# All four experts by pairs of chunks with seven block products, and the conversion steps spread along the experts

## The chip, the cores and the metric

The kernel runs on one core of one Trainium2 chip. The metric is the device time of one execution, in microseconds (us). The engines have the names of the profile: PE (matrix multiplication), PEld (its loading of stationary operands), DVE (vector engine), ACT (activation engine), POOL (GpSimd), and SP, whose queue issues nearly all transfers of this kernel.

## The reference, cut to what matters

```python
def reference(...):
    x = _attn_ref(q, k, v, n_global, n_local)      # banded attention, then [B*S, H*D] = [1536, 512]
    # experts: E = 4, D = 512, F = 1024
    p = domain_probs / (domain_probs.sum(-1, keepdims=True) + 1e-09)
    for e in range(E):
        h = np.maximum(x @ w1[e], 0.0)
        out += p[:, e:e + 1] * (h @ w2[e])
    # gate
    a = out @ w1_; b = out @ w2_
    return ((a * b) @ w3) @ w_out
```

All of it is fp32. The weights of the gate (w_ab, w3t, w_out) come to the kernel as 64-bit words that the kernel itself converts to fp32.

## The kernel before

**Products.** Every fp32 operand is split into a high and a low part (`split`, L48: ACT writes the high part, L50; DVE or POOL subtracts it to get the low one, L51). A product of two operands is three matmuls (`three`, L54: high by high, high by low, low by high, L56 to L58), each with a stationary block of 128x128 and 512 moving columns.

**Stages.** Attention comes first, then the experts, then the product of w3 with w_out, then the gate. The change is in the experts stage and in the conversion that runs beside it.

**The experts.** The 1536 tokens are three chunks c of 512, F is eight blocks f of 128. The loop over `work` (L831 on) takes steps (e, c, f): an up product of 12 matmuls into one of four `z` buffers, relu on ACT (L598) and its low part on DVE (L599), then the down product of the step before the last (`LAG` = 2), 12 matmuls into four `o` buffers that stay open over the eight f. After the eighth f the four `o` buffers are evacuated: DVE multiplies each by the shares of the expert (L804 or L807), and for a later expert POOL adds the result to `acc` (L808). The next group of downs can't start before that. Experts 0 and 1 (`EARLY` = 2) have all three chunks in `work`; experts 2 and 3 have chunk 0 there, 64 steps in all.

**The pairs.** Chunks 1 and 2 of experts 3 and 2, in that order, are done by `Pairs.run` (L705 to L740), one unit for two blocks f and both chunks: eight units n = 0 to 7. The 2x2 block product of a unit is made from seven products P1 to P7 of 6 matmuls each, where eight would be needed directly, from sums of x (made once, L654) and sums of weights (made for each unit, four DVE operations at L700, called the sums below, and their split with the low parts on POOL). The sums of the products are seven DVE adds that read `z` (L707) and one ACT copy (L719). In the program the unit stands as P1, P2, down group D0, P3, P4, D1, P5, D2, P6, D3, P7. The four `z` buffers go round, so a product takes the buffer of the fourth product before it. `prep(0)` after P2 splits the raw weights of the next unit (low parts on POOL), `prep(1)` after P4 makes its sums, `prep(2)` splits the second half of the weights on DVE (not for the first expert of the pairs). `out` writes relu and its low part for four results of the unit. A unit inside an expert has two downs of 12 matmuls (in D0 and D2), so 42 + 24 = 66 matmuls; one that starts another expert (n = 4) has the last two downs of chunk 1 in D0 and the eight of chunk 2 in D1, D2, D3, so 42 + 120 = 162, and evacuates twice.

**The conversion.** Forty pieces of 512 words by 128 partitions. For each: fetch of the raw words (SP), `abs` on ACT (L537), max on POOL (L539, one input), four DVE operations (L545, L548, L551, L553), an add of two inputs on POOL (L554), and the transfer of the result back to device memory. One step of each piece in flight is taken per work step from n = 5 on, with three raw buffers; all of it ends in the work loop.

**Order.** All five engines run in the order in which the program issues (`ORDERED`): an instruction that waits holds up everything behind it on its engine, and an issue of a transfer on SP that waits for its buffer holds up later ones.

## Time and profile before

| | us |
|---|---|
| median of 3 runs (lowest, highest) | 821.35 (821.28, 822.04) |
| the profiled execution | 820.91 |
| its span in the trace | 818.7 |
| PE busy in it | 812.0 (99%) |
| DVE, POOL, ACT busy in it | 507.7 (62%), 318.1 (39%), 283.4 (35%) |
| work loop after attention, 81.5 to 415.9 of the span | 334.4 |
| the eight units of the pairs, 415.9 to 557.3 | 141.4 |

Times of rows are microseconds from the start of the span. A row of the timeline has the start, the duration (from the first to the last of the instructions counted behind the x), the engine, the line, the operation, what it writes and reads, and in brackets how long the engine had been idle before it and what ended that. PE's granted clock is 1.00 in all 40 slices of the span.

### The profile page before, as it was taken

The numbers are of one execution on the slowest core, as the hardware profiler recorded it, in microseconds if no ns is written. First come the engines' busy times: TensorE is split into PE (matmuls) and PEld (weight loads), VectorE is DVE, ScalarE is ACT, GpSimd is POOL, SyncE is SP. The second block draws the span as 40 slices with busy tenths as digits, with TensorE's granted clock in tenths as the row PEclk, the third lists the DMA queues.
The fourth block names the chain that finished last, engine by engine and source line by source line (L and its number), as shares of the span: only waits on it lengthen the run. The fifth ranks groups of instructions, "written<-read, shape, count | busy, mean of one in ns | idle before, by whom it ended". The sixth has DMA issues, their size and how long they took to land.

```text
span 818.7 us, 11030 instructions
## 1 busy us (share of the span) xinstructions
PE 812.0 (99%) x4004; PEld 670.2 (82%) x4005; DVE 507.7 (62%) x945; ACT 283.4 (35%) x591; POOL 318.1 (39%) x320
## 2 busy tenths in 40 slices
PE   9999999999999999999999999999999999999997
PEld 5888888888888888888888888888888888888886
DVE  8996455567655557778648573665543743887850
ACT  7996222124221223333324221332442432333210
POOL 7886034525356464642143351422390003333400
PEclk9999999999999999999999999999999999999999
DMA  9940343558353547643101101121533210201011
GB/s 270 289 124 2 121 143 112 167 161 258 127 162 116 167 151 244 214 139 102 39 26 52 40 26 65 52 65 35 184 103 103 78 52 26 102 27 52 0 46 61
DMA packets 38116, 88.10 MB, mean 108 GB/s; under 512 B 3674, under 2 KB 9866, under 8 KB 38054
## 3 DMA queue, kind: packets, MB, share of 16 engines
q1 hardware_dynamic: 37382, 86.79, 33.4%
q8 instruction: 33, 0.54, 0.3%
q10 hardware_dynamic: 672, 0.54, 0.3%
q14 instruction: 29, 0.24, 0.1%
HBM read 73.66 MB, written 13.66 MB: 107 GB/s over the span
## 4 chain that ended last, share of the span: by engine, by line
PE 97%; DMA 1%; DVE 1%; issue 0%; SPq 0%; ACT 0%; ACTq 0%; DVEq 0%
PE z L56 18%; PE z L58 18%; PE z L57 18%; PE o L57 12%; PE o L58 12%; PE o L56 12%; PE sp L251 2%; PE tp L290 2%; PE op L329 1%; PE op L330 1%; PE tp L177 1%; PE sp L290 1%; DMA wr<-in_w_moe_dram 1%; PE sp L56 0%; PE sp L58 0%; PE sp L57 0%
## 5 line engine op out<-in xcount | busy, mean ns | idle before, releaser
L58 PE MATMUL z<-xh,sl 128*128 128x512 f32 x428 | 166.6, 389 | 0.0
L57 PE MATMUL z<-xl,sh 128*128 128x512 f32 x428 | 166.5, 389 | 0.0
L56 PE MATMUL z<-xh,sh 128*128 128x512 f32 x428 | 166.5, 389 | 0.0
L554 POOL TENSOR_TENSOR cr<-cr,cb 128x512 f32<-128x512 f32 x40 | 51.6, 1290 | 126.6 <-issue 118.8
L58 PEld LDWEIGHTS z<-xh,sl 128*128 128x128 f32 x428 | 80.3, 188 | 17.1 <-DVE sl L51 0.2
L57 PEld LDWEIGHTS z<-xl,sh 128*128 128x128 f32 x428 | 80.3, 188 | 16.7
L56 PEld LDWEIGHTS z<-xh,sh 128*128 128x128 f32 x428 | 80.4, 188 | 16.6
L51 POOL TENSOR_TENSOR sl<-wr,sh 128x512 fp32r<-128x512 f32 (+1 forms) x32 | 32.1, 1024 | 146.5 <-ACT sh L50 146.5
L51 DVE TENSOR_TENSOR sl<-wr,sh 128x1024 fp32r<-128x1024 f32 (+1 forms) x57 | 70.5, 1242 | 23.8 <-ACT sh L50 22.9
L808 POOL TENSOR_TENSOR acc<-acc,t 128x512 f32<-128x512 f32 x36 | 49.2, 1401 | 85.7 <-DVE t L807 85.7
L50 ACT CAST sh<-wr 128x1024 fp32r<-128x1024 f32 (+2 forms) x89 | 70.6, 815 | 22.1 <-PE z L57 10.3
L539 POOL TENSOR_SCALAR ca<-ca 128x512 f32<-128x512 f32 x40 | 61.7, 1543 | 26.8 <-ACT ca L537 26.8
L707 DVE TENSOR_TENSOR t<-t,z 128x512 f32<-128x512 f32 x56 | 37.4, 679 | 32.0 <-PE z L58 27.7
L306 POOL TENSOR_TENSOR pt<-pt,r 128x232 f32<-128x232 f32 (+1 forms) x95 | 48.7, 545 | 8.4 <-DVE r L237 4.4
L56 PE MATMUL z<-sh,sh 128*128 128x512 f32 x120 | 46.7, 389 | 0.0
L57 PE MATMUL z<-sl,sh 128*128 128x512 f32 x120 | 46.7, 389 | 0.0
L58 PE MATMUL z<-sh,sl 128*128 128x512 f32 x120 | 46.7, 389 | 0.0
L277 ACT ACTIVATE pt<-t,negmax 128x232 f32<-128x232 f32 (+1 forms) x96 | 44.8, 473 | 4.5 <-DVE negmax L266 4.4
L51 POOL TENSOR_TENSOR sl<-t,sh 128x256 fp32r<-128x256 f32 (+1 forms) x24 | 23.0, 973 | 31.2 <-ACT sh L50 31.0
L56 PE MATMUL o<-h0h,sh 128*128 128x512 f32 x84 | 32.8, 390 | 0.0
L57 PE MATMUL o<-h0l,sh 128*128 128x512 f32 x84 | 32.7, 389 | 0.0
L58 PE MATMUL o<-h0h,sl 128*128 128x512 f32 x84 | 32.7, 389 | 0.0
(266 smaller groups left out, 1745.4 us busy)
## 6 DMA issues: line engine op xcount, KB each, us to landing
wr<-in_w_moe_dram SPq DMA_DIRECT2D x44, 512.0 KB, 3.4
raw<-in_w3t_dram SPq DMA_DIRECT2D x16, 512.0 KB, 4.0
raw<-in_w_ab_dram SPq DMA_DIRECT2D x16, 512.0 KB, 4.3
wr<-wab_d SPq DMA_DIRECT2D x16, 512.0 KB, 3.3
raw<-in_w_out_dram SPq DMA_DIRECT2D x8, 512.0 KB, 3.4
w3t_d<-cr SPq DMA_DIRECT2D x16, 256.0 KB, 2.5
wab_d<-cr SPq DMA_DIRECT2D x16, 256.0 KB, 2.2
wr<-w3t_d SPq DMA_DIRECT2D x8, 512.0 KB, 3.3
```

The source lines that it names most:

```text
L50: nc.scalar.copy(hi, src)
L51: (lo_engine or nc.vector).tensor_tensor(lo, src, hi.bitcast(F32), op=ALU.subtract)
L56: nc.tensor.matmul(out, wh, xh, start=start, stop=False)
L57: nc.tensor.matmul(out, wh, xl, start=False, stop=False)
L58: nc.tensor.matmul(out, wl, xh, start=False, stop=stop)
L277: nc.scalar.activation(st[u][gr][:, hh, 0:w], t[:, 0:w], AF.Exp, bias=nm, scale=-1.0, accum_out=st[u]["sums"][:, h : h + 1])
L290: nc.tensor.transpose(tp[:, hh, j], pt[:, 2 * half + hh, c], g.ident)
L306: nc.gpsimd.tensor_tensor(pt[:, hh, 0:w], pt[:, hh, 0:w], r[:, hh : hh + 1].to_broadcast([P, w]), op=ALU.mult)
L539: nc.gpsimd.tensor_scalar(a, a, 2.0**-15, None, op0=ALU.max)
L554: nc.gpsimd.tensor_tensor(rest, rest, top.bitcast(F32), op=ALU.add)
L707: add = lambda o, a, b: nc.vector.tensor_tensor(o, a, b, op=ALU.add)
L808: nc.gpsimd.tensor_tensor(acc[c][:, d], acc[c][:, d], t, op=ALU.add)
```

## The change

- `EARLY` is gone: `work` holds chunk 0 of all four experts (32 steps), and the pairs are experts 3, 2, 1, 0, so 16 units n = 0 to 15. Units 4, 8 and 12 start another expert.
- The sums of the weights for the next unit (`prep(1)`) stand before the add of P3 in every unit but 4, 8 and 12 (`early`), where they stay behind the add of P4.
- The conversion is a class, `Convert`, with two raw buffers and operations in place. A step starts a piece (abs, max), sends the result of an earlier one, ends the piece begun before (four DVE operations, POOL add), and fetches the next. The steps stand in a table of places: 12 in the work loop (`CONVERTS`), one inside an `out` of every unit but the last and 4, 8, 12 (`INSIDE`: between relu and its low part), five in each of the units 4, 8, 12 and one more at the end of unit 4 (`BETWEEN`: after a down), and three in the downs after the last unit (`ENDS`).
- Weights of the work steps are fetched up to two slots ahead (`load_more`, `land_until`); in steps 8 to 11 two slots are split per step where one was.
- The sums of x are made in six given work steps (`XSUMS`). For chunks 1 and 2 expert 3 now writes `acc` directly, and expert 0 for chunk 0 as before. A scratch area for transfers is made smaller.

```diff
@@ -35,8 +35,12 @@
 WARM = 10
 FILL = (6, 4)
 W_TILE = 4
-EARLY = 2
 LAG = 2
+XSUMS = (21, 23, 24, 26, 27, 28)
+CONVERTS = (4, 6, 7, 8, 10, 11, 12, 13, 14, 18, 20, 22)
+ENDS = (2, 4, 6)
+BETWEEN = [(4, 3, 0)] + [(n, j, m) for n in (4, 8, 12) for j, m in ((0, 0), (1, 0), (1, 1), (2, 0), (2, 1))]
+INSIDE = [(n, 1, 1) for n in range(15) if n not in (4, 8, 12)]
 BIG = 1.0e30
 MASKED = -1.0e9
 
@@ -537,22 +541,44 @@
     nc.scalar.activation(a, high.bitcast(F32), AF.Abs)
 
     nc.gpsimd.tensor_scalar(a, a, 2.0**-15, None, op0=ALU.max)
-    return low, high, a.bitcast(I32)
+    return low, high, a
 
 
 def convert_end(nc, pool, low, high, a):
 
-    nc.vector.tensor_scalar(a, a, 3, 0x3FFFFFF8, op0=ALU.logical_shift_left, op1=ALU.bitwise_and)
-
-    top = pool.tile([P, 512], I32, name="cb", bufs=1)
-    nc.vector.scalar_tensor_tensor(top, high, -0x40000000, a, op0=ALU.bitwise_and, op1=ALU.bitwise_or)
-
-    pw = pool.tile([P, 512], I32, name="cp", bufs=1)
-    nc.vector.tensor_scalar(pw, top, -0x800000, None, op0=ALU.bitwise_and)
-    rest = pool.tile([P, 512], F32, name="cr")
-    nc.vector.scalar_tensor_tensor(rest, low.bitcast(U32), 2.0**-52, pw.bitcast(F32), op0=ALU.mult, op1=ALU.mult)
-    nc.gpsimd.tensor_tensor(rest, rest, top.bitcast(F32), op=ALU.add)
+    top, rest = a.bitcast(I32), pool.tile([P, 512], F32, name="cr")
+    nc.vector.tensor_scalar(top, top, 3, 0x3FFFFFF8, op0=ALU.logical_shift_left, op1=ALU.bitwise_and)
+    nc.vector.scalar_tensor_tensor(top, high, -0x40000000, top, op0=ALU.bitwise_and, op1=ALU.bitwise_or)
+    nc.vector.tensor_scalar(rest.bitcast(I32), top, -0x800000, None, op0=ALU.bitwise_and)
+    nc.vector.scalar_tensor_tensor(rest, low.bitcast(U32), 2.0**-52, rest, op0=ALU.mult, op1=ALU.mult)
+    nc.gpsimd.tensor_tensor(rest, rest, a, op=ALU.add)
     return rest
+
+
+class Convert:
+
+
+    def __init__(self, nc, pool, pieces):
+        self.nc, self.pool, self.pieces = nc, pool, list(pieces)
+        self.fetched, self.begun, self.ended = [], [], []
+
+    def step(self):
+        nc = self.nc
+        if self.fetched:
+            raw, dst = self.fetched.pop(0)
+            self.begun.append((convert_start(nc, self.pool, raw), dst))
+        if self.ended:
+            nc.sync.dma_start(*self.ended.pop(0))
+        if len(self.begun) > 1 or not self.pieces and self.begun:
+            piece, dst = self.begun.pop(0)
+            self.ended.append((dst, convert_end(nc, self.pool, *piece)))
+            if not self.begun:
+                nc.sync.dma_start(*self.ended.pop(0))
+        while self.pieces and len(self.fetched) + len(self.begun) < 2:
+            src, dst = self.pieces.pop(0)
+            raw = self.pool.tile([P, 512], mybir.dt.int64, name="raw")
+            nc.sync.dma_start(raw, src)
+            self.fetched.append((raw, dst))
 
 
 class Ring:
...
-        self.work = [(e, c, f) for e in range(E) for c in range(NCH if e < EARLY else 1) for f in range(FC)]
+        self.work = [(e, 0, f) for e in range(E) for f in range(FC)]
         self.pending, self.ahead = {}, 0
 
     def up(self, w, z, later=False):
...
-    def out(self, w, z, to):
+    def out(self, w, z, to, between=None):
 
         nc = self.nc
         hh, hl = to
         nc.scalar.activation(hh, z, AF.Relu)
+        if between:
+            between()
         nc.vector.scalar_tensor_tensor(hl, z, 0.0, hh.bitcast(F32), op0=ALU.max, op1=ALU.subtract)
         self.pending[w] = (hh, hl)
 
@@ -720,11 +748,15 @@
         add(s6, s1, product("s2", "t2"))
         prep(0)
         issue(0)
+        early = n % (FC // 2) or not n
+        if early:
+            prep(1)
         add(s1, s1, product("a12", "b21"))
         out(0, 1, s1)
         u3 = tmp()
         add(u3, s6, product("s3", "t3"))
-        prep(1)
+        if not early:
+            prep(1)
         issue(1)
         z = product("s1", "t1")
         c22 = tmp()
@@ -752,8 +784,8 @@
         acc = [big.tile([P, KC, CW], F32, name=f"acc{c}") for c in range(NCH)]
         of_experts = ExitStack()
         xp = of_experts.enter_context(tc.tile_pool(name=name + "xp", bufs=1))
-        late = ExitStack()
-        cpool = late.enter_context(tc.tile_pool(name=name + "cv", bufs=2))
+        tpool = of_experts.enter_context(tc.tile_pool(name=name + "xt", bufs=1))
+        cpool = of_experts.enter_context(tc.tile_pool(name=name + "cv", bufs=2))
         ring = experts.ring
         if not first_time:
             for key in list(ring.of):
...
-        pieces = list(g.pieces) if first_time else []
-
-        pairs = list(range(E - 1, EARLY - 1, -1))
+        convert = Convert(nc, cpool, g.pieces if first_time else [])
+
+        pairs = list(range(E - 1, -1, -1))
...
@@ -800,7 +832,7 @@
             ring.give((e, c, f))
             if f == fs[-1]:
                 for d in range(KC):
-                    if e == 0:
+                    if e == (pairs[0] if c else 0):
                         nc.vector.tensor_tensor(acc[c][:, d], o[d], state["p"], op=ALU.mult)
                         continue
                     t = tmp()
@@ -815,29 +847,38 @@
         ctx.enter_context(tc.manual_schedule(engines=ORDERED))
 
         ready, done = (4, len(pending)) if first_time else (0, 0)
-        for f in range(ready, ready + 2):
-            load_slot(f, g.w_moe[0, f])
+        todo = [(f, g.w_moe[e, f]) for e, c, f in work][ready:]
+
+        def load_more():
+
+            while todo and len(coming) < 2:
+                load_slot(*todo.pop(0))
+
+        def land_until(n):
+
+            while coming and len(work) - len(todo) - len(coming) <= n:
+                land(len(coming) - 1)
+            load_more()
+
+        load_more()
         if not first_time:
             land(1)
-            load_slot(2, g.w_moe[0, 2])
+            load_more()
         if first_time:
-            room = cpool.tile([P, 512], mybir.dt.int64, name="raw", bufs=3).bitcast(F32)
+            room = cpool.tile([P, 512], mybir.dt.int64, name="raw").bitcast(F32)
             nc.sync.dma_start(
                 room[: N // P, 0 : E * P].rearrange("c (t e) -> c t e", e=E), g.probs.rearrange("(c t) e -> c t e", t=P)
             )
-        fetched, begun, ended = [], [], []
-        by_pairs = raws = xsums = None
-        first_pair = len(work) - 2 * FC
+        by_pairs = Pairs(nc, tpool, tmp, ps_z, experts)
+        xsums = by_pairs.sums_of_x()
         for n, w in enumerate(work):
             if n >= done:
                 experts.up(w, ps_z.tile([P, CW], F32, name="z"))
-                if n >= FC:
-                    land()
-                elif coming:
-                    s = coming[-1][0] + 1
+                if n < FC:
                     land(len(coming) - 1)
-                    if s < FC:
-                        load_slot(s, g.w_moe[0, s])
+                    load_more()
+                elif n % FC != LAG - 1:
+                    land_until(n + FC - LAG - 1)
...
@@ -848,29 +889,11 @@
             if n >= LAG:
                 e, c, f = work[n - LAG]
                 down(e, c, f)
-
-                if e + 1 < E and (e >= EARLY or c == NCH - 1):
-                    load_slot(f, g.w_moe[e + 1, f])
-            if n > 4 and n % FC != LAG - 1:
-                if ended:
-                    nc.sync.dma_start(*ended.pop(0))
-                if begun:
-                    piece, dst = begun.pop(0)
-                    ended.append((dst, convert_end(nc, cpool, *piece)))
-                if fetched:
-                    raw, dst = fetched.pop(0)
-                    begun.append((convert_start(nc, cpool, raw), dst))
-                if pieces:
-                    src, dst = pieces.pop(0)
-                    raw = cpool.tile([P, 512], mybir.dt.int64, name="raw", bufs=3)
-                    nc.sync.dma_start(raw, src)
-                    fetched.append((raw, dst))
-            if by_pairs is None and n >= first_pair and not (pieces or fetched or begun or ended):
-                late.close()
-                tpool = of_experts.enter_context(tc.tile_pool(name=name + "xt", bufs=1))
-                by_pairs = Pairs(nc, tpool, tmp, ps_z, experts)
-                xsums = by_pairs.sums_of_x()
-            elif xsums:
+                if n >= FC and n % FC == LAG - 1:
+                    land_until(n + FC - LAG - 1)
+            if n in CONVERTS:
+                convert.step()
+            if n in XSUMS:
                 next(xsums, None)
...
@@ -898,8 +921,10 @@
                 downs = [work[-LAG:], [], [], []]
 
             def issue(j):
-                for e, c, f in downs[j]:
+                for m, (e, c, f) in enumerate(downs[j]):
                     down(e, c, f, order.get(c))
+                    if (n, j, m) in BETWEEN:
+                        convert.step()
 
...
@@ -923,13 +948,15 @@
                 else:
 
                     to = x_hi[2][:, f - 4], x_lo[2][:, f - 4]
-                experts.out((e, c, f), z, to)
+                experts.out((e, c, f), z, to, convert.step if (n, row, c) in INSIDE else None)
 
             by_pairs.run(n, issue, prep, out)
 
         order[2] = [7, 4, 0, 1, 2, 3, 5, 6]
-        for e, c, f in [w for d in ends(pairs[-1]) for w in d]:
+        for n, (e, c, f) in enumerate([w for d in ends(pairs[-1]) for w in d]):
             down(e, c, f, order[c], tail=c == 2)
+            if n in ENDS:
+                convert.step()
...
@@ -1295,7 +1322,7 @@
         "w3t": words(by_rows(moe2_w3.T)),
         "w_out": words(moe2_w_out.reshape(4, 2, P, DM).transpose(0, 2, 1, 3).reshape(4, P, 2 * DM)),
     }
-    nc = _bacc.Bacc("TRN2", target_bir_lowering=False, num_devices=1)
+    nc = _bacc.Bacc("TRN2", target_bir_lowering=False, num_devices=1, dynamic_dma_scratch_size=512)
```

PE has 8148 rows in the program before and 8052 in the one after: 48 matmuls and 48 loads of stationary blocks fewer. Three places, with the rows as they stand in the program:

DVE in unit 6, from the add of P2 on (`t<-t,z` are the adds of products, `t<-wr` the sums of the weights, `h2l` a low part), before:

```order
L707 TENSOR_TENSOR t<-t,z 128x512 x2
L599 SCALAR_TENSOR_TENSOR h2l<-t,h2h 128x512
L707 TENSOR_TENSOR t<-t,z 128x512
L700 TENSOR_TENSOR t<-wr 128x256
L700 TENSOR_TENSOR t<-t,wr 128x256
L700 TENSOR_TENSOR t<-wr 128x256
L700 TENSOR_TENSOR t<-wr,t 128x256
L707 TENSOR_TENSOR t<-t,z 128x512 x2
```

and after:

```order
L735 TENSOR_TENSOR t<-t,z 128x512
L728 TENSOR_TENSOR t<-wr 128x256
L728 TENSOR_TENSOR t<-t,wr 128x256
L728 TENSOR_TENSOR t<-wr 128x256
L728 TENSOR_TENSOR t<-wr,t 128x256
L735 TENSOR_TENSOR t<-t,z 128x512
L627 SCALAR_TENSOR_TENSOR h2l<-t,h2h 128x512
L735 TENSOR_TENSOR t<-t,z 128x512 x3
```

The four sums moved from behind the add of P4 to before the add of P3.

DVE at the head of a unit that starts another expert (`t<-o_...,prob` evacuate the four `o` buffers), unit 4 before:

```order
L707 TENSOR_TENSOR t<-t,z 128x512
L807 TENSOR_TENSOR t<-o_4343,prob 128x512
L807 TENSOR_TENSOR t<-o_4344,prob 128x512
L807 TENSOR_TENSOR t<-o_4345,prob 128x512
L807 TENSOR_TENSOR t<-o_4346,prob 128x512
L707 TENSOR_TENSOR t<-t,z 128x512
L599 SCALAR_TENSOR_TENSOR h2l<-t,h2h 128x512
L707 TENSOR_TENSOR t<-t,z 128x512
```

and unit 8 after:

```order
L735 TENSOR_TENSOR t<-t,z 128x512
L550 TENSOR_SCALAR ca<-ca 128x512
L551 SCALAR_TENSOR_TENSOR ca<-raw,ca 128x512
L552 TENSOR_SCALAR cr<-ca 128x512
L553 SCALAR_TENSOR_TENSOR cr<-raw,cr 128x512
L839 TENSOR_TENSOR t<-o_3630,prob 128x512
L839 TENSOR_TENSOR t<-o_3631,prob 128x512
L839 TENSOR_TENSOR t<-o_3632,prob 128x512
L839 TENSOR_TENSOR t<-o_3633,prob 128x512
L735 TENSOR_TENSOR t<-t,z 128x512
L627 SCALAR_TENSOR_TENSOR h3l<-t,h3h 128x512
L735 TENSOR_TENSOR t<-t,z 128x512
```

The four operations of a conversion stand ahead of the evacuation.

ACT in the later part of such a unit (`h.h` and `xh` are relus, `sh` casts of weights, `ca<-raw` the abs that starts a conversion), unit 4 before:

```order
L598 ACTIVATE xh_70<-t 128x512
L50 CAST sh_76<-wr 128x512
L50 CAST sh_78<-wr 128x512
L598 ACTIVATE h0h<-t 128x512
L598 ACTIVATE xh_70<-t 128x512
L719 COPY t<-z 128x512
```

and unit 8 after:

```order
L541 ACTIVATE ca<-raw 128x512 x2
L624 ACTIVATE xh_70<-t 128x512
L54 CAST sh_76<-wr 128x512
L54 CAST sh_78<-wr 128x512
L541 ACTIVATE ca<-raw 128x512 x2
L624 ACTIVATE h2h<-t 128x512
L624 ACTIVATE xh_70<-t 128x512
L747 COPY t<-z 128x512
```

Two abs that read fetched raw words stand ahead of a relu, at two points of the unit.

## Rows read from the trace of the kernel before

**Rows 1.** The page, busy time by engine: us, share of span, instructions.
```profile
PE 812.0 (99%) x4004; PEld 670.2 (82%) x4005; DVE 507.7 (62%) x945; ACT 283.4 (35%) x591; POOL 318.1 (39%) x320
```

**Rows 2.** Windows: stretch, length, busy of PE, PEld, DVE, ACT, POOL, clock, DMA share, GB/s.
```profile
81.50:415.90 334.40, 334.40 (x1477) 276.50 (x1476) 208.14 (x322) 92.67 (x143) 139.02 (x101) 1.00 0.47 150
415.90:557.30 141.40, 141.12 (x624) 116.57 (x623) 87.00 (x133) 42.93 (x81) 49.26 (x47) 1.00 0.14 44
```

**Rows 3.** Timeline of PE, first matmuls of units 0, 6 and 7.
```profile
415.96 0.39 PE L56 MATMUL z<-xh,sh 128*128 128x512 f32 x1
...
528.02 0.39 PE L56 MATMUL z<-xh,sh 128*128 128x512 f32 x1
...
542.99 0.39 PE L56 MATMUL z<-xh,sh 128*128 128x512 f32 x1
```

**Rows 4.** Timeline of PEld, between P1 and P2 of unit 1.
```profile
431.83 0.19 PEld L58 LDWEIGHTS z<-xh,sl 128*128 128x128 f32 x1
432.69 0.19 PEld L56 LDWEIGHTS z<-t2h,sh 128*128 128x128 f32 x1 [0.67 <-ACT xh L598]
```

**Rows 5.** Timeline of DVE, unit 6 to the same place of unit 7.
```profile
532.37 0.68 DVE L707 TENSOR_TENSOR t<-t,z 128x512 f32<-128x512 f32 x1
...
535.02 0.69 DVE L707 TENSOR_TENSOR t<-t,z 128x512 f32<-128x512 f32 x1 [1.98 <-PE z L58]
536.41 0.69 DVE L599 SCALAR_TENSOR_TENSOR h2l<-t,h2h 128x512 fp32r<-128x512 f32 x1 [0.70 <-ACT h2h L598]
...
537.62 0.42 DVE L700 TENSOR_TENSOR t<-wr 128x256 f32<-128x256 f32 x1
...
538.75 0.97 DVE L700 TENSOR_TENSOR t<-wr,t 128x256 f32<-128x256 f32 x1
...
542.09 1.28 DVE L51 TENSOR_TENSOR sl<-wr,sh 128x512 fp32r<-128x512 f32 x2
...
547.26 0.68 DVE L707 TENSOR_TENSOR t<-t,z 128x512 f32<-128x512 f32 x1
```

**Rows 6.** Timeline of ACT, unit 6 (a relu).
```profile
535.75 0.63 ACT L598 ACTIVATE h2h<-t 128x512 fp32r<-128x512 f32 x1 [2.72 <-DVE t L707]
```

**Rows 7.** Timeline of POOL, unit 6 (low parts of raw weights, then of sums).
```profile
532.85 1.99 POOL L51 TENSOR_TENSOR sl<-wr,sh 128x512 fp32r<-128x512 f32 x2 [6.12 <-ACT sh L50]
538.61 0.82 POOL L51 TENSOR_TENSOR sl<-t,sh 128x256 fp32r<-128x256 f32 x1 [3.77 <-ACT sh L50]
```

**Rows 8.** Timeline of DVE, unit 0, evacuation and what follows.
```profile
422.29 2.80 DVE L807 TENSOR_TENSOR t<-o,prob 128x512 f32<-128x512 f32 x4 [2.64 <-PE o L58]
...
427.13 1.57 DVE L599 SCALAR_TENSOR_TENSOR h0l<-t,h0h 128x512 fp32r<-128x512 f32 x1 [0.76 <-ACT h0h L598]
```

**Rows 9.** Timeline of POOL, unit 0.
```profile
423.12 5.03 POOL L808 TENSOR_TENSOR acc<-acc,t 128x512 f32<-128x512 f32 x4 [2.42 <-DVE t L807]
430.15 3.09 POOL L51 TENSOR_TENSOR sl<-t,sh 128x256 fp32r<-128x256 f32 x3 [2.00 <-ACT sh L50]
```

**Rows 10.** Timeline of DVE, work loop: a split, a conversion, the next split.
```profile
175.71 1.23 DVE L51 TENSOR_TENSOR sl<-wr,sh 128x1024 fp32r<-128x1024 f32 x1 [0.25 <-ACT sh L50]
176.85 0.42 DVE L545 TENSOR_SCALAR ca<-ca 128x512 int32<-128x512 int32 x1
...
178.50 0.69 DVE L553 SCALAR_TENSOR_TENSOR cr<-raw,cp 128x512 f32<-128x512 uint32 x1
...
181.15 1.22 DVE L51 TENSOR_TENSOR sl<-wr,sh 128x1024 fp32r<-128x1024 f32 x1 [0.25 <-ACT sh L50]
```

**Rows 11.** Timeline of POOL, beside rows 10.
```profile
179.33 1.29 POOL L554 TENSOR_TENSOR cr<-cr,cb 128x512 f32<-128x512 f32 x1 [4.17 <-issue]
180.59 1.48 POOL L539 TENSOR_SCALAR ca<-ca 128x512 f32<-128x512 f32 x1
```

**Rows 12.** The page, DMA issues: engine, operation, count, KB each, median us to landing.
```profile
raw<-in_w3t_dram SPq DMA_DIRECT2D x16, 512.0 KB, 4.0
```

**Rows 13.** The same of the window from 300 to 410 alone.
```profile
raw<-in_w_ab_dram SPq DMA_DIRECT2D x7, 512.0 KB, 5.3
```

## The prediction

> **What bounds the kernel now.** I read the busy times first [rows 1]: PE is busy 99% of the span, the others 62% or less. So the kernel is as long as PE's stream, and a change gains only by matmuls that go, and loses only where PE has to wait. The windows by stage [rows 2] are next: PE has no gap in the work loop, and 141.12 of 141.40 us in the eight units of the pairs, where DVE is busy 87.0 (62%). PE's first matmuls of units 6 and 7 [rows 3] give its pitch: 542.99 - 528.02 = 14.97 us for the 66 matmuls of a unit, 0.2268 us each (the 0.39 of a row overlaps with its neighbours). The one gap is between P1 and P2 of unit 1, where the load of the first sums stands idle 0.67 us [rows 4]; the missing 0.28 of the window and the 0.67 bound what it costs, and I take 0.4.
>
> Then DVE across one unit [rows 5]. From the add of P2 in unit 6 (532.37) to that of unit 7 (547.26) is 14.89 us, and DVE waited for PE in 1.98 of it. So it has 2 us to spare per unit; the add stands 532.37 - 528.02 = 4.35 us behind the unit's start on PE. That distance, called L below, grows when DVE falls behind, and PE stops where it needs a buffer that DVE empties.
>
> **What the change removes.** Eight more units in the seven-product form, 6 matmuls fewer in each: 48 x 0.2268 = 10.89 us, all of it on PE. The order shows 48 fewer, so that the change might not do what it says is no open question. The gap of unit 1 goes too, since the sums come earlier: 0.4. That is 820.91 - 10.89 - 0.4 = 809.62, if PE never waits for anything new.
>
> **What it adds: the lock.** In unit 0 a low part on DVE took 1.57 us from 427.13 [rows 8] where the same operation took 0.69 in unit 6, and its end, 428.70, follows the end of POOL's four acc adds, 423.12 + 5.03 = 428.15, by 0.55 [rows 9]. The last of the sums took 0.97 rather than 0.42 [rows 5] beside POOL's low part that started at 538.61 [rows 7]. So a DVE operation with two inputs in SBUF waits for the end of a two-input operation of POOL, and a POOL operation for DVE's in turn. A split on DVE that started in the middle of POOL's max (180.59 to 182.07) took 1.22 [rows 10, 11], as much as one with POOL idle (1.23). So the max, with one input, holds up nobody.
>
> The Trainium skill, "SBUF — State Buffer", section "SBUF: two separate sides", says that DVE and GpSimd share a port pair as an exclusive lock, held for the whole instruction, and that a DVE operation with two SBUF inputs is kept off it by any GpSimd operation that reads SBUF. The trace agrees for two-input operations of POOL and differs for the max. What the max would cost by that rule is a rival below.
>
> **A unit inside an expert.** DVE's need in unit 6 is 14.89 - 1.98 = 12.91. A conversion is added: from 176.85 to 178.50 + 0.69 is 2.34, of which 2.24 is the pitch once the next operation overlaps [rows 10]. It stands in the wait of DVE for a relu, 0.70 [rows 5], itself 0.63 of ACT [rows 6], so 1.54 is added. The sums now stand beside the two low parts of raw weights on POOL, 1.99 [rows 7], and meet one after the other: each can wait for an operation of about 1 us. They took 538.75 + 0.97 - 537.62 = 2.10; I take 3.6, so 1.5 more (bounds 0 and 3). Sum: 15.95 against 14.97 of PE. DVE loses 1.0 a unit, and L grows from 4.35 to about 7.3 in three. The first expert of the pairs lacks the two splits of 1.28 [rows 5], so there a unit needs 14.7 and DVE keeps up. A PE stall inside these units needs L above about 7.5: an add that frees a `z` comes three products later. Cost here 0.2.
>
> **Unit 0.** The sums now stand right behind the evacuation, which ends at 422.29 + 2.80 = 425.09 [rows 8], while POOL's acc adds run to 428.15 [rows 9]. Four sums that alternate with acc adds of 1.26 (5.03 / 4) end at about 425.1 + 4 x 1.2 = 429.9. Then the add of P3, relu, low part and the add of P4, 0.6 + 0.1 + 0.7 + 0.7 + 0.6 = 2.7, end at 432.6. That add frees the buffer for unit 1's P1, which PE wants at 415.96 + 14.97 = 430.93 [rows 3]. PE waits 1.7 (bounds 0.5, with half the waits, and 2.1).
>
> **Units 4, 8 and 12.** No unit of before holds a conversion and an evacuation, so this is bounded from rows of other places: below by 0, since DVE's work (two evacuations of 2.8, five conversions of 2.24, seven adds of 0.6, four low parts of 0.7 with a relu's wait of 0.7, sums 2.1 and splits 1.3: 30) is less than the 162 x 0.2268 = 36.7 of PE; above by 4, two waits for a landing [rows 12] on the path, less half of it hidden. The middle goes as follows. In units 8 and 12 a conversion stands ahead of the evacuation. From the add of P2: 0.6, the conversion 2.24, 1.5 for its two-input operations behind POOL's low parts [rows 7], and 0.7 for the first buffer, so `o` comes free at L + 5.05. D1 wants it 48 matmuls behind the unit's start, at 10.89. PE waits as soon as L is over 5.85; with L = 7.3 it waits 1.4. At the end of the unit the last conversion is led by a chain: the piece before it is ended on DVE, its raw buffer is fetched anew, 4.0 [rows 12], then abs on ACT, with the relu of the fourth result behind it, low part, evacuation. With L = 4.35 that ends 2.9 us before the next unit's D0 wants `o` (36.7 + 2.7 = 39.4 behind the unit's start). DVE is 1.5 late still (7.3 - 4.35 - 1.4), and in two pairs of back-to-back conversions the second meets the first one's POOL add of 1.29 [rows 11], about 1.2 each: 3.9 of delay, so PE waits 1.0 more. That is 2.4 for each of 8 and 12. In unit 4, L is still 4.35 and POOL has no acc adds, but a sixth conversion stands between the last two downs, whose raw words are fetched only when the fourth is done; I take 1.5. Bounds 0 and 4 each.
>
> **Hidden.** In the work loop steps 8 to 11 split two slots each, 1.22 more of DVE [rows 10], where a step of PE has 24 x 0.2268 = 5.4; before, DVE had 208 of 334 us [rows 2]. Cost 0 (bound 3, four times a split of 0.75 uncovered). The 8 MB more of weights come in a stage where the transfers were at 14% [rows 2]. The conversions of the tail have several downs of 2.7 us on either side.
>
> **The sum.** 809.62 + 1.7 + 1.5 + 2 x 2.4 + 0.2 = 817.8 for a profiled execution. That of before was 820.91 and the median 821.35, 0.44 more, so 818.3 for the median.
>
> **Rivals.**
> 1. *DVE keeps up.* If the sums beside POOL cost 2.1 to 2.5 rather than 3.6, L stays near 4.35, and of the stalls about 1.5 is left, most of it in unit 0: 809.62 + 1.5 + 0.44 = 811.6; without any stall 810.1. For it: 2 us of slack per unit [rows 5] and a unit's need only just over its time. Against it: every sum of before that met POOL was slowed [rows 5].
> 2. *ACT stands behind raw words* (the slower side). Where the transfers were dense, raw words took 5.3 us to land, not 4.0 [rows 13]. With two raw buffers a fetch waits for a conversion to end, two abs stand ahead of a relu at two points of each of the units 4, 8, 12, and ACT can't pass them. Two landings of 1.3 more in three units, with the slack used up, cost 7.8: 818.3 + 7.8 = 826.1. It decides from a landing of about 5 us. For it: a unit now moves three transfers of 512 KB and one of 256 KB in 15 us, some 120 GB/s, nearer to the 150 of the work loop than to the 44 of the pairs before [rows 2]. Against it: those in the work loop were 4.0 in the median [rows 12].
> 3. *The max locks DVE too.* A DVE operation would wait half of the 1.48 [rows 11] on average, less the overlap, say 0.6, in each of 28 conversions of the pairs: 17 us on a DVE that has no time left, 818.3 + 17 = 835. Against it: the split of 1.22 [rows 10].
> 4. *The doubled splits of steps 8 to 11 aren't covered*: 3 more, 821.3.
>
> **How the numbers follow.** About 0.2% is what a measurement of this kernel can tell from no change, so faster is under 819.7 and slower over 823.0. My forecast, 818.3, has 0.46, with its own range from 814 to 823 by the bounds of the stalls: 0.30 faster, 0.14 the same, 0.02 slower. Rival 1, 0.28, is faster. Rival 2, 0.18: 0.03 the same, 0.15 slower. Rival 3, 0.04, slower; rival 4, 0.04, the same. Together 0.58 faster, 0.21 the same, 0.21 slower. The range of 8 in 10 takes in the forecast and most of rival 1, down to 811, and about half of rival 2, up to 825.
>
> **What would show it.** PE has 48 matmuls fewer and the pitch stays 0.2268. Right: the sums next to POOL take 3 us or more; the add of P2 goes from some 4.4 behind its unit's start to 6 to 7 over units 5 to 7; the first loads of D1 in units 8 and 12 wait for an evacuation, P1 of unit 1 for an add. Rival 1: PE is idle under 2 us in all in the 16 units. Rival 2: abs on ACT idle behind raw words, with a relu behind. I'm wrong if PE waits elsewhere, in the work loop or the tail, or if L doesn't grow.

## The result, and the profile after

The changed kernel takes 831.35 us in the median (831.13 to 833.59) against 821.64 of the kernel before: a ratio of 1.0124, 95% interval 1.0106 to 1.0142. It is slower by 1.2%, where 818.3 was forecast and 811 to 825 allowed. The profiled execution took 831.13 us, of which 829.3 are the span, 10.6 more than before (818.7). The mean granted clock was 0.999 in it and 0.995 to 0.996 in the other three executions, one of which took 833.59.

The page, busy time by engine, beside [rows 1], and two windows of the trace (columns as in [rows 2]): the work loop, and the sixteen units up to the last product.

```profile
PE 805.5 (97%) x3956; PEld 659.1 (79%) x3957; DVE 615.0 (74%) x1049; ACT 315.0 (38%) x655; POOL 382.2 (46%) x360
```

```profile
81.50:241.60 160.10, 160.10 (x708) 131.98 (x707) 113.88 (x154) 57.73 (x82) 53.73 (x34) 1.00 0.52 163
241.60:567.00 325.40, 308.53 (x1339) 249.27 (x1338) 281.29 (x395) 108.48 (x205) 192.81 (x151) 1.00 0.36 116
```

PE still has no gap in the work loop. In the units DVE is busy 281.3 of 325.4 us, 86%, where it was 62% before [rows 2], and PE has gaps. Who ended them, for PE's waits from 240 to 570 (total, times, longest):

```profile
PE o L60 <- DVE t L839: 7.2, 4, 2.4
PE o L60 <- DVE acc L836: 4.1, 2, 2.7
PE z L60 <- DVE t L735: 3.5, 6, 0.8
PE o L61 <- DVE h2l L627: 1.1, 1, 1.1
PE o L61 <- DVE h3l L627: 1.1, 1, 1.1
```

All are waits for DVE: for evacuations (L836, L839), for adds that free a `z` buffer (L735), and for low parts of the hidden layer (L627). The gaps between the starts of matmuls, over the pitch of 0.2268, add up to 21.1 us in the units (before: 0.5 in the eight, nothing else behind attention). So the span is 818.7 - 10.9 - 0.5 + 21.1 = 828.4. The 0.9 that is missing to 829.3 lies in pieces too small for that count: from the first matmul of unit 0 (241.59) to the end of unit 15 (568.39) it is 326.8 us, 22.0 more than 1344 x 0.2268 = 304.8. One gap of each kind in PE's timeline (the start is that of the matmul that had waited):

```profile
255.96 0.50 PE L60 MATMUL z<-xh,sh 128*128 128x512 f32 x1 [0.61 <-DVE t L735]
...
315.87 0.50 PE L60 MATMUL o<-h3h,sh 128*128 128x512 f32 x1 [1.36 <-DVE acc L836]
...
347.48 0.47 PE L60 MATMUL o<-h2h,sh 128*128 128x512 f32 x1 [2.72 <-DVE acc L836]
...
397.08 0.50 PE L61 MATMUL o<-h2l,sh 128*128 128x512 f32 x1 [1.08 <-DVE h2l L627]
...
471.36 0.50 PE L60 MATMUL z<-t3h,sh 128*128 128x512 f32 x1 [0.55 <-DVE t L735]
```

In order: P7 of unit 0 (P1 of unit 1 waits likewise), D1 of unit 4 (and of 8 and 12), D0 of unit 5 (and of 9 and 13), the second down of D0 in unit 8 (and a down of D0 in 12), P4 of unit 11. Each idle time is 0.16 short of what the start is late by. By place the 21.1 are 1.95 at unit 1, 4.6 at unit 4 and the D0 behind it, 5.9 at unit 8, 5.0 at unit 12, and 3.2 at P4 of units 10, 11, 14 and 15 (0.8 each); the rest is in pieces of 0.1.

**Where DVE's time goes inside an expert.** DVE's timeline from the add of P2 of unit 6 to that of unit 7, answering to [rows 5]:

```profile
366.99 0.68 DVE L735 TENSOR_TENSOR t<-t,z 128x512 f32<-128x512 f32 x1
367.59 1.40 DVE L728 TENSOR_TENSOR t<-wr 128x256 f32<-128x256 f32 x1
...
370.67 0.41 DVE L728 TENSOR_TENSOR t<-wr,t 128x256 f32<-128x256 f32 x1
371.01 0.68 DVE L735 TENSOR_TENSOR t<-t,z 128x512 f32<-128x512 f32 x1
...
382.95 0.68 DVE L735 TENSOR_TENSOR t<-t,z 128x512 f32<-128x512 f32 x1
```

The unit takes DVE 382.95 - 366.99 = 15.96 us, with no wait for PE left in it, against 14.97 of PE; the four sums take 371.08 - 367.59 = 3.49, where they took 2.10 before [rows 5].

**And at a change of expert.** DVE in unit 8, from its add of P2 to that of unit 9:

```profile
398.99 0.68 DVE L735 TENSOR_TENSOR t<-t,z 128x512 f32<-128x512 f32 x1
399.59 1.41 DVE L550 TENSOR_SCALAR ca<-ca 128x512 int32<-128x512 int32 x1
401.03 1.11 DVE L551 SCALAR_TENSOR_TENSOR ca<-raw,ca 128x512 int32<-128x512 int32 x1
...
402.93 0.69 DVE L553 SCALAR_TENSOR_TENSOR cr<-raw,cr 128x512 f32<-128x512 uint32 x1
403.54 2.48 DVE L839 TENSOR_TENSOR t<-o,prob 128x512 f32<-128x512 f32 x4
...
413.24 1.40 DVE L552 TENSOR_SCALAR cr<-ca 128x512 int32<-128x512 int32 x1
...
417.17 1.51 DVE L550 TENSOR_SCALAR ca<-ca 128x512 int32<-128x512 int32 x1 [1.38 <-POOL ca L543]
...
430.55 0.43 DVE L552 TENSOR_SCALAR cr<-ca 128x512 int32<-128x512 int32 x1 [0.88 <-DMA wab_d<-cr]
...
431.62 0.68 DVE L735 TENSOR_TENSOR t<-t,z 128x512 f32<-128x512 f32 x1
434.10 0.69 DVE L627 SCALAR_TENSOR_TENSOR h2l<-t,h2h 128x512 fp32r<-128x512 f32 x1 [1.80 <-ACT h2h L624]
434.71 2.48 DVE L839 TENSOR_TENSOR t<-o,prob 128x512 f32<-128x512 f32 x4
...
439.35 0.67 DVE L735 TENSOR_TENSOR t<-t,z 128x512 f32<-128x512 f32 x1
```

That is 40.4 us for a unit in which PE has 162 x 0.2268 = 36.7 of work. The operations of a conversion took 0.42, 0.69, 0.43 and 0.69 when alone; here rows show 1.41, 1.11, 1.40, 1.51. Summed over the stretch, operations of DVE are prolonged by 8.9 us over their quiet times, and DVE waits 4.1 for a max that stood on POOL behind low parts, for a transfer out, and for a relu that ACT holds back. ACT shows why, in the same unit:

```profile
432.88 0.66 ACT L541 ACTIVATE ca<-raw 128x512 f32<-128x512 f32 x1 [7.83 <-DMA raw<-in_w_ab_dram]
433.45 0.61 ACT L624 ACTIVATE h2h<-t 128x512 fp32r<-128x512 f32 x1
```

The abs stood 7.83 us waiting for its raw words, and the relu, whose add had ended at 432.3 (431.62 + 0.68), behind it. The fetch itself was late: SP issued it 2.6 us into that wait, right behind the conversion that frees the buffer, and from there to the abs it is 5.2 us.

```profile
427.66 0.33 SPq L580 DMA_DIRECT2D raw<-in_w_ab_dram  x1
```

### The profile page after: what moved, and what is told of

Its sections match the earlier page's. It is cut to its first block, busy times and chain, and to the rows that moved or that the text cites. A ratio compares the mean times of both kernels' runs of the same rounds, so it can differ in the third digit from the quotient of the medians.

```text
span 829.3 us, 11170 instructions
## 1 busy us (share of the span) xinstructions
PE 805.5 (97%) x3956; PEld 659.1 (79%) x3957; DVE 615.0 (74%) x1049; ACT 315.0 (38%) x655; POOL 382.2 (46%) x360
## 4 chain that ended last, share of the span: by engine, by line
PE 64%; DVE 22%; ACT 4%; issue 4%; DMA 3%; POOL 2%; SPq 0%; DVEq 0%; ACTq 0%; POOLq 0%
PE z L60 13%; PE z L62 12%; PE z L61 12%; PE o L60 6%; PE o L62 6%; PE o L61 6%; DVE t L728 5%; DVE t L735 5%; PE sp L255 2%; DVE ca L551 2%; DVE cr L553 2%; DMA raw<-in_w_ab_dram 2%; DVE sl L55 2%; DVE ca L550 2%; PE tp L294 2%
## 5 line engine op out<-in xcount | busy, mean ns | idle before, releaser
L60 PE MATMUL z<-xh,sh 128*128 128x512 f32 x348 | 135.9, 391 | 1.4 <-DVE t L735 1.4
L62 PE MATMUL z<-xh,sl 128*128 128x512 f32 x348 | 135.5, 389 | 0.0
L61 PE MATMUL z<-xl,sh 128*128 128x512 f32 x348 | 135.5, 389 | 0.0
L55 POOL TENSOR_TENSOR sl<-wr,sh 128x512 fp32r<-128x512 f32 (+1 forms) x48 | 50.8, 1080 | 134.6 <-ACT sh L54 129.8
L54 ACT CAST sh<-wr 128x1024 fp32r<-128x1024 f32 (+2 forms) x121 | 87.0, 749 | 38.1 <-DMA wr<-in_w_moe_dram 13.7
L735 DVE TENSOR_TENSOR t<-t,z 128x512 f32<-128x512 f32 x112 | 74.7, 679 | 5.6 <-PE z L62 4.1
L554 POOL TENSOR_TENSOR cr<-cr,ca 128x512 f32<-128x512 f32 x40 | 57.6, 1439 | 15.7 <-DVE cr L553 15.7
L55 POOL TENSOR_TENSOR sl<-t,sh 128x256 fp32r<-128x256 f32 (+1 forms) x48 | 53.0, 1119 | 20.6 <-ACT sh L54 20.2
L541 ACT ACTIVATE ca<-raw 128x512 f32<-128x512 f32 x40 | 26.7, 668 | 63.1 <-DMA raw<-in_w_ab_dram 30.6
L54 ACT CAST sh<-t 128x256 fp32r<-128x256 f32 (+1 forms) x48 | 21.9, 478 | 54.4 <-DVE t L728 54.4
```

The source lines that it names most:

```text
L54: nc.scalar.copy(hi, src)
L55: (lo_engine or nc.vector).tensor_tensor(lo, src, hi.bitcast(F32), op=ALU.subtract)
L60: nc.tensor.matmul(out, wh, xh, start=start, stop=False)
L61: nc.tensor.matmul(out, wh, xl, start=False, stop=False)
L62: nc.tensor.matmul(out, wl, xh, start=False, stop=stop)
L554: nc.gpsimd.tensor_tensor(rest, rest, a, op=ALU.add)
```

## The experiments

Theory A is the prediction's mechanism at another size: DVE is full in the units, from the conversions, their locks with POOL and the early sums, and PE waits for it. The rivals blame one part alone: the sums, the place of the conversions, the landing of raw words, or the add on POOL. An experiment without an interval is one execution; the four of the changed kernel lie 2.5 us apart, so differences of that size are read from the traces and not from the times.

**Whose work fills DVE.** First the conversions of the pairs were left out as a whole, and then only those of the units that change the expert.

```diff
         assert next(xsums, None) is None
+        convert.step = convert.lite      # sends a converted piece, no other work
...
```

> The changed kernel with the conversions left out from the end of the work loop on (30 of the 40 pieces: no fetch, no abs, no max, no DVE operations, no add; an already converted piece is sent in their place, so the results behind it are not those of the reference). Theory A (DVE is full in the pairs, and the conversions with their locks fill it): without them a unit needs 14 to 14.5 us of DVE against 14.97 of PE, the add of P2 falls back to 3 to 4 us behind its unit's start, and of the 21.2 us that PE waits only the 2 at unit 1 are left: about 812 us. Rival B (the sums beside POOL's low parts are enough to hold PE up): PE still waits 8 us or more: 818 or above.

812.26 us, as theory A has it. PE waits twice in the units, for an add, 1.4 us together. These are the two waits at unit 1, 2.0 us of lost matmul time. The add of P2 stands 3.0 us behind its unit's start (L) in all units from 3 on.

```diff
-                    if (n, j, m) in BETWEEN:
-                        convert.step()
+                    if (n, j, m) in BETWEEN and convert.pieces:
+                        convert.lite()
```

> The changed kernel with the 16 conversions in units 4, 8 and 12 left out (an already converted piece is sent instead), those inside the other units kept. Theory A, with the change units as the place where DVE's lag is made: L falls back to about 4 in them, the three units behind them use that up at 1 us each, PE waits 2 at unit 1 and 0 to 3 in all the rest: 812 to 815. If the conversions inside the units are the main cost, PE still waits 8 to 10: 820.

811.93 us, with the same 2.0 of waits as without any conversion. So the sixteen pieces in units 4, 8 and 12 carry all the rest of the loss, 19 of 21 us, and the conversions inside the other units cost nothing as long as these three give DVE time to catch up: L is 3.0 in unit 5, then 4.6, 5.7 and 6.8 in the three that follow, and 3.1 in unit 9, behind the next change.

**Which of the pieces at a change.**

```diff
                     if (n, j, m) in BETWEEN:
-                        convert.step()
+                        (convert.step if j < 2 or not convert.pieces else convert.lite)()
```

> The changed kernel with the last conversions of units 4, 8 and 12 left out (both in D2, and the one in D3 of unit 4: seven pieces, a converted one is sent instead); the three in D0 and D1 stay. If the lag is made by these last ones, the waits at the next unit's D0 (3.0, 2.6, 1.7) go, L falls to about 4 behind the change, and with it the waits inside units 6 to 15; 1.6 at unit 4 and about 1 at 8 and 12 stay: 817 to 819. If the first three fill DVE just as much, the waits only move: 824 or more.

818.51 us. Of 21.2 us of waits 7.8 are left: 2.0 at unit 1, and the rest at D1 of units 4, 8, 12 and one low part. The seven late pieces are worth 12.8 us, more than the 7.3 of the D0 that wait for the late evacuation: L is 3.0 and 4.7 in units 5 and 9, not 9.1, and with that the waits inside the units that follow are gone too.

**Order, or amount.**

```diff
-BETWEEN = ... for j, m in ((0, 0), (1, 0), (1, 1), (2, 0), (2, 1))]
+BETWEEN = ... for j, m in ((0, 1), (1, 0), (1, 1), (2, 0), (2, 1))]
```

> The changed kernel with the first conversion of units 4, 8 and 12 one down later, so that the four evacuating operations stand ahead of it on DVE. The waits of D1 in these units (1.6, 1.9, 1.9) should go. If DVE's total work through the unit decides, as theory A says, the time comes back at the next unit's D0 and little is gained: 827 to 831. If the place alone decided, the 5.4 us are gained: 825.7.

833.37 us, above both ranges. The waits of D1 are gone, and come back at the next D0: 4.6 to 4.7 each for 3.0, 2.6 and 1.7. All waits together are 17.9 us, 3.3 less than in the changed kernel, and yet PE loses more, 24.1 us for 21.2 by the starts of its matmuls. The windows behind the first two of these waits show why (columns as before, the last but two is the granted clock):

```profile
347.80:357.80 10.00, 10.00 (x33) 7.98 (x34) 8.57 (x13) 3.90 (x8) 5.62 (x6) 0.72 0.29 90
436.70:446.70 10.00, 9.98 (x33) 8.05 (x34) 8.84 (x11) 3.69 (x8) 10.00 (x9) 0.73 0.00 0
```

33 matmuls in 10 us, and 35 behind the third wait (clock 0.78), where 44 fit: 2.0 to 2.5 us each, 6 to 7 in all, behind a wait. More on the clock below.

**Landing.**

```diff
             src, dst = self.pieces.pop(0)
...
+            if not fetch:                # in units 4, 8, 12
+                self.fetched.append((used, dst))
+                continue
             raw = self.pool.tile([P, 512], mybir.dt.int64, name="raw")
```

> The changed kernel in which the conversion steps in units 4, 8 and 12 fetch nothing: each next piece is made from the raw words that already lie in the buffer (its words are those of an earlier piece). All engine work is as in the changed kernel, only the landing of raw words, and abs on ACT that stands waiting for it ahead of relus, is gone. If work and locks on DVE alone make the loss: 829 to 831. If ACT behind raw words is a part of it (the second rival), each change of expert is shorter by 2 to 4: 821 to 825.

826.26 us: 5.1 less, between the two ranges. The fetch and landing of raw words, with ACT standing ahead of a relu, are a part of the loss, a quarter, and almost all of it at the next unit's D0 (1.9 in all for 7.3). The low parts, the D1 waits and those at P4 stay as they were.

**The add on POOL.**

```diff
-    nc.gpsimd.tensor_tensor(rest, rest, a, op=ALU.add)
     return rest
```

> The changed kernel without the POOL add that ends each conversion (L554 left out, so the converted words lack that term). If the lock between DVE and two-input operations of POOL is a good part of the loss, DVE gets back the some 10 us by which its operations were prolonged beside this add: 4 to 8 us less, 823 to 827. If the loss is DVE's own work alone (2.24 a conversion), nothing changes: 830 to 832.

828.18 us, 3.2 less, just short of the range given. The waits fall from 21.2 to 17.1. The lock with this add is a part, and a small one.

**The early sums.**

```diff
-        early = n % (FC // 2) or not n
+        early = False
```

> The changed kernel with the sums of the weights behind the add of P4 in every unit, as in the kernel before. Theory A: DVE is spared 1.5 us of lock in each unit, which then needs 14.5 instead of 15.97, so it catches up between the changes of expert; unit 1 waits 0.4 instead of 1.95; the units 4, 8 and 12 still lose 2 to 3 each: about 818 us. Rival C (the sums stand early because late ones would not have their low parts in time for P2): PE waits at P2 in most units and the time is 831 or more.

822.65 us, 8.7 less, though 4.7 over what was expected. The sums take 2.09 again:

```profile
367.97 0.42 DVE L728 TENSOR_TENSOR t<-wr 128x256 f32<-128x256 f32 x1
...
369.10 0.96 DVE L728 TENSOR_TENSOR t<-wr,t 128x256 f32<-128x256 f32 x1
```

L stays at 6.0 in units 6, 7 and 8, where it had grown by a microsecond each; P2 waits only once, 0.4 at unit 1, so rival C falls. The D0 behind each change still waits 2.4 to 2.8, which leaves the crowded end of the change as its cause. Behind two of these three waits the clock fell to 0.83 and 0.84 over 10 us, 37 and 38 matmuls for 44.

Is it the lock with the low parts on POOL, or the place in DVE's order? DVE's order was kept, and the low parts of the raw weights put behind the sums:

```diff
-                if j == 0 and n < last:
+                if j == 0 and n < last and not early:
                     by_pairs.split_w(n + 1, raws.here[0])
                 if j == 1 and n < last:
                     by_pairs.sums_of_w(n + 1, raws.here[0])
+                    if early:
+                        by_pairs.split_w(n + 1, raws.here[0])
...
```

> The changed kernel with DVE's order as it is (sums early), but with the split of the next unit's raw weights, casts on ACT and low parts on POOL, behind the sums instead of ahead of them, in all units but 4, 8 and 12. If the 3.5 us that the early sums take (2.1 late) is the lock with those low parts, the sums take 2.1 to 2.5 again; the low parts then meet the one relu low part and the add behind them, so a unit inside an expert needs 14.6 to 15.4 rather than 16.0, and PE waits less: 822 to 827. If it is the place of the sums in DVE's order that costs, nothing changes: 830 to 832.

832.57 us: the first half came out as expected, the second didn't. DVE in unit 6:

```profile
368.57 0.42 DVE L728 TENSOR_TENSOR t<-wr 128x256 f32<-128x256 f32 x1
...
369.69 0.97 DVE L728 TENSOR_TENSOR t<-wr,t 128x256 f32<-128x256 f32 x1
...
372.50 1.82 DVE L627 SCALAR_TENSOR_TENSOR h2l<-t,h2h 128x512 fp32r<-128x512 f32 x1 [1.24 <-ACT h2h L624]
...
383.94 0.68 DVE L735 TENSOR_TENSOR t<-t,z 128x512 f32<-128x512 f32 x1
```

The same four sums at the same place take 2.1 us, so what prolonged them was POOL's low parts. But the unit still takes 383.94 - 367.97 = 15.97 (the add of P2 stands at 367.97): the relu now waits behind the casts of the split (1.24 for 0.70), and its low part meets POOL and takes 1.82 for 0.69. The lock wasn't removed, it moved to the next operation with two inputs in SBUF. Late sums avoid it because POOL is idle where they begin: in the run with late sums from 366.8 to 368.9, and the sums begin at 368.0.

**Both remedies.** Late sums, six more conversions in the work loop, three at a change.

```diff
+        early = False
+CONVERTS = (4, 5, 6, 7, 8, 10, 11, 12, 13, 14, 15, 16, 18, 19, 20, 22, 24, 29)
+BETWEEN = [(n, j, 1) for n in (4, 8, 12) for j in (0, 1, 2)]
```

> The changed kernel with the sums of the weights late in every unit, six more conversions in the work loop (steps 5, 15, 16, 19, 24, 29), and three rather than five in units 4, 8, 12, behind the second down of D0, D1 and D2; all forty pieces are converted. Theory A: DVE keeps up in every unit, PE waits 0.4 at unit 1 and less than 1 elsewhere: 810 to 811.5, 1.3% less than the kernel before. If the work loop has no room for six more, or the low parts of late sums come too late: 815 or more.

821.86 us in the median, a ratio to the kernel before of 1.0011 (1.0001 to 1.0021). The units went as theory A has it, 0.4 of wait in all sixteen. But the work loop had no room at the steps chosen: PE waits there twice, 7.8 us together, where it waited for nothing before. The windows behind the two waits:

```profile
172.20:182.20 10.00, 9.98 (x37) 8.12 (x38) 9.90 (x10) 3.27 (x4) 10.00 (x7) 0.83 0.54 181
222.00:232.00 10.00, 9.99 (x34) 8.05 (x35) 9.28 (x10) 1.92 (x3) 6.93 (x4) 0.75 0.46 148
```

Ahead of the first, a step with a conversion lasts some 5.7 on DVE (from one split at 160.61 to the next at 166.30), over the 24 x 0.2268 = 5.44 of PE. Seven in a row (steps 10 to 16) add up until DVE's evacuation comes too late: its first operation ends at 172.07, and the down that needs the buffer starts at 172.22. (The profile puts this wait down to a relu that ended at 172.10, but the down reads an older hidden block.) Of the 5.7 only 5.3 is DVE's own time, locks included. In the rest it waits for ACT, which in these steps stands 3.1 to 3.9 us before an abs for its raw words, ahead of a relu and a cast. So late raw words have a part in it, and no run separates them from DVE's work.

So the conversions were put where DVE had been busy under 2.7 us of a step.

```diff
+        early = False
+CONVERTS = (4, 5, 6, 7, 8, 10, 11, 12, 13, 14, 18, 20, 22, 29, 30, 31)
+BETWEEN = [(n, j, m) for n in (4, 8, 12) for j, m in ((0, 1), (1, 0), (1, 1), (2, 1))]
```

> The changed kernel with the sums late in every unit, four conversions more in the work loop but at its two ends, where DVE was busy under 2.7 of 5.44 us a step (steps 5, 29, 30, 31), and four in units 4, 8, 12: behind the second down of D0, the first two of D1 and the second of D2. All forty pieces are converted. If DVE's work and the order of its work are all there is to the loss, PE waits 0.4 at unit 1 and under 1.5 elsewhere, never for 4 us at once, and the clock stays at 1.00: 810 to 812, 1.2 to 1.3% less than before. If the fourth conversion is too many, each of units 5, 9, 13 waits 1 to 3 at D0: 813 to 820.

810.51 us, a ratio to the kernel before of 0.9873 (0.9856 to 0.9889): by the medians 1.3% under the kernel before and 2.5% under the changed one. Its two windows, and all that PE waits for from 80 to 700:

```profile
81.50:242.20 160.70, 160.70 (x710) 132.24 (x709) 122.58 (x165) 59.13 (x84) 59.18 (x38) 1.00 0.55 174
242.20:547.50 305.30, 304.91 (x1346) 252.15 (x1345) 259.59 (x386) 109.29 (x205) 179.50 (x147) 1.00 0.37 118
```

```profile
PE z L60 <- ACT xh L624: 0.4, 1, 0.4
```

DVE is busy 85% of the sixteen units, as much as in the changed kernel (86%), and PE waits for next to nothing: 305 us rather than 325, with four conversions fewer in the units and otherwise the same work. The equal shares mislead, since each is taken of its own time, stalls included. Of the 304.8 that PE's matmuls need, DVE's busy time is 92% in the changed kernel (281.3) and 85% here (259.6). The four conversions are about 9 of that difference by an estimate (4 x 2.24); the rest fits operations that wait less for POOL.

The same places with early sums:

> The same places of the conversions with the early sums of the changed kernel. Theory A: L is 7.1 at unit 4 and grows by 1.0 a unit behind each change, and a change unit with four conversions gives little of it back: unit 1 waits 1.95, the next units' D0 1 to 3 each, some 6 to 9 in all: 815 to 819. If it is the crowding of conversions at the change alone that costs, and early sums are harmless: 812 to 813.

817.28 us, with 7.0 of waits: 2.0 at unit 1, little at units 4 to 9, 0.3 at unit 10, and 0.5 to 1.3 a unit from unit 11 on, when L has come to 8.9. So of the 20.8 us between the changed kernel and the best one the places of the conversions give 14.1 and the late sums another 6.8; the late sums alone gave 8.7.

## Why the prediction was wrong, by its steps

- **What is removed.** Right. PE has 48 matmuls fewer and keeps its pitch; with no waits but those at unit 1 the time is 811.9, with late sums 810.5, where 809.62 + 0.44 = 810.1 was worked out for no stall at all.
- **Unit 0.** Right in mechanism and nearly in size: 1.7 predicted, 1.95 measured, on P1 of unit 1 and P7 before it (0.9 of it), both for adds behind the sums.
- **A unit inside an expert.** Right: 15.95 predicted for DVE, 15.96 measured; 14.7 for the first expert, 14.8 measured; sums of 3.6, 3.49 measured. The limit of L was put too low, 7.5; P4 begins to wait at about 8.1 (0.1 late with L at 8.16 in unit 7, 0.6 to 0.7 with L at 8.7 to 8.9 in units 10, 11, 14 and 15). The waits inside these units, 0.2 predicted, are 3.2 in P4, because L passed that limit.
- **The step that failed** is L at the two ends of a change. "In unit 4, L is still 4.35": it was 7.1. Unit 0 left an L of 7.7 behind in unit 1, and units of 14.8 against 14.97 give back only 0.1 to 0.2 each (7.7, 7.5, 7.2, 7.1). I had put a number on the delay of unit 0 and on the slack of the units behind it, and didn't carry the one into the other. The first matmul and the add of P2 of unit 4, and of unit 5 behind the change:

```profile
303.48 0.39 PE L60 MATMUL z<-xh,sh 128*128 128x512 f32 x1
...
310.58 0.68 DVE L735 TENSOR_TENSOR t<-t,z 128x512 f32<-128x512 f32 x1
...
341.88 0.39 PE L60 MATMUL z<-xh,sh 128*128 128x512 f32 x1
...
351.02 0.68 DVE L735 TENSOR_TENSOR t<-t,z 128x512 f32<-128x512 f32 x1
```

- **A second part of it, the larger,** is the term for units 4, 8 and 12. I set DVE's work at 30 and its delays at 3.9, against 2.9 to spare at the end of the unit, and so let L begin anew at 4.35 behind each change. DVE took 40.4 us in unit 8: the prolonged operations were 8.9, the waits for a max, a transfer and a relu 4.1. L was 9.1 behind unit 4 as well as behind unit 8 (351.02 - 341.88, and 439.35 less the start of unit 9 at 430.28). Predicted 1.5, 2.4 and 2.4 for the three; measured 4.6, 5.9 and 5.0, over the bound of 4 that I gave each. That bound held two landings on the path and no lock; the run without the fetches shows that fetch and landing are 5 of the 21 us.
- **A term that was missing.** In units 8 and 12 the second down of D0 waited 1.3 for a low part. The conversion inside unit 7 stands between relu and its low part, and I had counted that on DVE alone, not for the down that reads it.
- **Rivals.** The first (DVE keeps up) is refuted for this kernel and is what the best version does. The second (ACT behind raw words) would have given 826.1; its mechanism is there, with an abs waiting 7.83 us and a fetch of 5.2, and its share is the 5.1 us of the run without the fetches. It was no alternative to the forecast's mechanism but came on top of it. The third (the max locks DVE) is there at less than half its size, 6.7 us of DVE's time where 17 was put; more below. The fourth, doubled splits, is refuted: no gap in the work loop.
- **The slower side** was given 0.21, most of it (0.15) to one rival with a landing as its cause. It should have been the case in which DVE simply doesn't recover between two changes. The check for that was at hand: three units at a loss of 1.0 and a change unit must together be within PE's time, and I bounded the change unit from below by DVE's work without locks.

## What to carry to other kernels

When an engine off the critical path is filled up, carry its lag from stage to stage as a running balance, unit by unit, and let it fall only by slack that is shown; a stall threshold means little without that balance. The work moved into the cover must be priced in the company that it will have: the same conversion took 2.2 us of DVE alone and up to 4 beside POOL and a transfer out. A busy share that is taken of a time with stalls in it hides how full an engine is: at 86% and 85% PE waited 21 us or under 1. What decides is that the added work stands where the engine has its slack, neither in runs nor between a result and the engine that waits for it, and that two-input operations stand where the other engine of the lock is idle.

## What the runs showed of the hardware

**The lock.** The max on POOL did hold up operations of DVE, those that begin early in it. DVE and POOL in unit 7 of the changed kernel:

```profile
395.44 0.98 DVE L553 SCALAR_TENSOR_TENSOR cr<-raw,cr 128x512 f32<-128x512 uint32 x1
396.35 0.68 DVE L627 SCALAR_TENSOR_TENSOR h2l<-t,h2h 128x512 fp32r<-128x512 f32 x1
```

```profile
395.26 1.50 POOL L543 TENSOR_SCALAR ca<-ca 128x512 f32<-128x512 f32 x1 [5.36 <-ACT ca L541]
```

The max ran from 395.26 to 396.76; the operation at 395.44 took 0.98 for 0.69, the low part at 396.35 its usual 0.68. In the units, 19 operations of L553 began while a max ran. The 14 that began in its first 0.25 us took 0.98 to 1.13 and ended 0.33 before the max did; the five that began 0.9 us or more into it took 0.69, as with POOL idle (the row at 402.93 above is one). No low part or split with two inputs in SBUF began less than 0.47 into a max, so their usual times don't show that they are exempt. In the last experiment (early sums, conversions at the ends) a sum did, and took 0.83 for 0.42:

```profile
238.76 0.83 DVE L728 TENSOR_TENSOR t<-wr 128x256 f32<-128x256 f32 x1
```

```profile
238.47 1.72 POOL L543 TENSOR_SCALAR ca<-ca 128x512 f32<-128x512 f32 x1 [1.82 <-ACT ca L541]
```

So as far as these rows go, the max holds up an operation of these kinds that begins in about its first half microsecond, and none that begins later. The prediction's "holds up nobody" rested on a split that began 0.56 into it. In the sixteen units that comes to 6.7 us of prolonged operations. The Trainium skill, "SBUF — State Buffer", section "SBUF: two separate sides", has the loser of the port pair blocked for the whole instruction: that agrees with the two-input operations of POOL (the sums, 3.49 for 2.1), and not with the max. A DVE operation with one input in SBUF waits for the two-input operations too: L550 took 1.41 for 0.42.

**The clock.** In the profiled execution of the changed kernel, with waits of up to 2.9 us, the granted clock is 1.00 over the 10 us behind each of the longest. Behind the waits of 3.6 us and more, five in two kernels, it is 0.72 to 0.83 there, and matmuls go at a pitch of some 0.43 for a while, the lower of two levels (1.2 and 2.4 GHz). Behind a wait of 4.55 us:

```profile
347.76 0.77 PE L60 MATMUL o<-h2h,sh 128*128 128x512 f32 x1 [4.38 <-DVE acc L836]
348.33 0.63 PE L61 MATMUL o<-h2l,sh 128*128 128x512 f32 x1
348.76 0.63 PE L62 MATMUL o<-h2h,sl 128*128 128x512 f32 x1
```

Waits between 2.4 and 2.9 were followed by such a stretch in some runs and not in others: two of three with late sums (0.83 and 0.84), three of three with the sums ahead of the low parts (0.83 each), and neither of two in the changed kernel. The windows behind a wait of 2.9 in the changed kernel and in the run with the sums ahead of the low parts:

```profile
347.50:357.50 10.00, 10.00 (x44) 8.28 (x45) 8.56 (x13) 3.90 (x8) 5.62 (x6) 1.00 0.27 88
```

```profile
348.50:358.50 10.00, 10.00 (x37) 8.10 (x38) 8.03 (x13) 3.90 (x8) 5.39 (x6) 0.83 0.16 53
```

What decides there isn't settled by these runs. Before each, PE had run at full speed. A wait with such a stretch behind it costs some 1.6 to 2.5 us over its own length, so the kernel with 17.9 us of waits lost more of PE's time than the one with 21.2.
